# First chunk of a local-and-strided attention with a two-matrix MLP: local exponentials kept in PSUM, copies on another engine, a new order of the opening steps

## The chip, the core and the metric

The kernel runs on one core of a Trainium2 chip. The metric is the device time of one execution in microseconds (us). Three executions of the kernel before took 881.85, 885.22 and 885.75 us; their median is 885.22 us.

## What is computed

```python
scores = q @ k.T / sqrt(64)                       # 8 batches, 8 heads, 576 positions
mask   = local (0 <= i-j < 32) for heads 0..3, strided (i-j >= 0, i%32 == j%32) for heads 4..7
attn   = exp(scores - max); attn = attn / (sum(attn) + 1e-9)
x      = (attn @ v)                               # 4608 tokens x 512
h      = maximum(x @ w_in, 0)                     # 512 x 2048
out    = (h * h) @ w_out                          # 2048 x 512
```

All of it is float32. Products of the MLP are made from split operands: each number is a high part in a rounded format plus the remainder, and a product is three matmuls (high·high, high·low, low·high).

## The kernel before

The 4608 tokens go in twelve chunks of 384. A chunk's MLP has sixteen steps: `up(c, j)` makes 128 rows of h with twelve matmuls of 384 columns (L462), and `down(c, j)` adds them into three PSUM banks with nine matmuls of 512 columns (L489). While TensorE works on chunk c, the other engines prepare the attention of chunk c+1. Between `up` and `down` stand: a relu (L470 in the first chunk), the square (L471, VectorE), the high part `gh` (L475, ScalarE) and the low part `gl` (L476, VectorE).

Nothing can run beside the attention of the first chunk, so it is written apart. Its eight heads are four pairs, each a generator `pe_pair`: `first[0]` and `first[1]` are the local pairs, `late[0]` and `late[1]` the strided ones. A step of a pair runs up to the next `yield`:

1. loads of q and k, then of v (SP's queue);
2. scores by TensorE (L319) and, per window of 96 queries, the negated masked maximum by VectorE (L324, here called a minimum; it also writes the masked scores to SBUF, tile `e`);
3. exponentials and sums. A local pair is `single`: eight ScalarE instructions with an accumulated sum each (L345). A strided pair has its maximum subtracted by GpSimd (L347), two exponentials (L348) and a reduction by VectorE (L349). Then a reduction (L350), a reciprocal (L351) and the division, a multiplication by GpSimd (L353);
4. transposes by TensorE (L359) into the PSUM banks that held the scores, copied to SBUF by ScalarE (L360);
5. the product with v (L367, L378) and the split of the result into x's high part (L382, ScalarE) and low part (L383, VectorE).

The weights arrive as raw pairs of words, 1 MB a tile. `fetch` loads a tile, `convert` turns it into high and low parts in halves of 512 columns: `scale` (L154, ScalarE, 1024 columns), then per half z (L166, ScalarE), a merge (L169, VectorE), the high part (L172, ScalarE) and the low part (L173, GpSimd). L172 and L173 of a half are issued only in the next half's step (`split`).

The order of the opening steps is written by hand (L588 to L628), and a scheduler places instructions of the steps among each other within it, by its own estimate; each engine then runs its own list in order. `issue_after` and `behind` keep what follows behind an instruction. `zeros(bank, n)` issues n matmuls on a tile of zeros into a bank that nobody reads.

Access to a PSUM tile is guarded by the whole bank: a write to one window of it waits for reads of the others.

Of the kernel before, what the change touches and what calls it, by code (L numbers as in the profile page):

```python
# [22 lines left out]
P = 128  # L23
# [63 lines left out]
def attn_moe(ctx: ExitStack, tc, qk_l, v_l, qk_d, v_d, qk_p, v_p, f_s, q_s, k_s, v_s, w_in, w_out, masks, eye, out):  # L87
# [59 lines left out]
    def convert():  # L147
# [9 lines left out]
        for k in range(NFT):  # L157
# [4 lines left out]
            for raw, at in cuts:  # L162
# [8 lines left out]
                def split(w=w, hi=hi, lo=lo, at=at, k=k):  # L171
                    last["a"] = nc.scalar.copy(hi, f32(w))  # L172
                    last["g"] = nc.gpsimd.tensor_sub(lo, f32(w), f32(hi))  # L173
                    if at and 4 <= k < 12:
                        fetch(k + 4)

                if not at and k + 1 < NFT and k + 1 in raws:
                    with tc.issue_after(first_step.ins):
                        scale(k + 1)
# [112 lines left out]
    def pe_pair(c, pr, local, qk, vr, es, pt, banks, sm, single):  # L292
# [22 lines left out]
        s_ps = [banks() for _ in range(2)] if c == 0 else None  # L315
        e4 = [e[:QC, : NW * kw].rearrange("p (w k) -> p w k", k=kw) for e in es]
        def scores(h, w, s):
# [10 lines left out]

        if s_ps:
            for w in range(NW):  # L330
                for h in range(2):
                    scores(h, w, s_ps[h])
# [9 lines left out]
        for h in range(2):  # L342
            if single:
                for w in range(NW):
                    last["a"] = nc.scalar.activation(e4[h][:, w], e4[h][:, w], AF.Exp, bias=nm[:QC, h, w : w + 1], scale=-1.0, accum_out=ss[:QC, NW * h + w, :1])  # L345
            else:
# [5 lines left out]
        for h in range(2):  # L352
            last["g"] = nc.gpsimd.tensor_mul(e4[h], e4[h], rs[:QC, h].unsqueeze(2).broadcast_to([QC, NW, kw]))  # L353
        yield
        p4 = pt.rearrange("p (h w q) -> p h w q", h=2, w=NW)
        for h in range(2):
            t = s_ps[h] if s_ps else banks()
            for w in range(NW):
                nc.tensor.transpose(t[:kw, w * QC : (w + 1) * QC], e4[h][:, w], ident[:QC, :QC])  # L359
            last["a"] = nc.scalar.copy(pt[:kw, h * TC : (h + 1) * TC], t[:kw, :TC])  # L360
        yield
# [241 lines left out]
    with tc.issue_after(last["p"].ins):  # L603
        zeros(0, NWARM // 2)
        for k in range(NEARLY, 8):
            fetch(k)
    next(late[0])
    with tc.issue_after(last["p"].ins):
        zeros(1, NWARM // 2)
    next(first[0])  # L610
    next(first[1])
    weights = behind({"a": last["a"]}, ungated)
    next(late[1])
    for i in range(2):
        next(first[0])
        next(first[1])
        next(late[0])
        next(late[1])
        if i:
            weights = behind({"a": last["a"]}, ungated)  # L620
        for _ in range(2):
            next(weights)
    next(late[0])
    next(late[1])
    for _ in range(2 * NEARLY - 4):
        next(weights)
# [131 lines left out]
```

## Time and profile before

| | |
|---|---|
| median of three executions | 885.22 us |
| the profiled execution: time | 883.18 us |
| the profiled execution: span from first to last instruction | 881.4 us |
| mean granted TensorE clock, share of full | 0.997 |
| TensorE matmuls, share of the span | 99% |
| VectorE | 72% |
| ScalarE | 65% |
| GpSimd | 77% |

The profiled execution lies between the three timed ones, 2.0 us under their median. Busy shares are means over the whole run; the opening, the first chunk and the eleven others have different limits, so the rows that count are those of the first 50 us. Times in rows are us from the start of the span. TensorE's busy share counts pipelined matmuls from issue to end.

### The profile page before, as it was taken

The numbers are of one execution on the slowest core, as the hardware profiler recorded it, in microseconds if no ns is written. First come the engines' busy times: TensorE is split into PE (matmuls) and PEld (weight loads), VectorE is DVE, ScalarE is ACT, GpSimd is POOL, SyncE is SP. The second block draws the span as 40 slices with busy tenths as digits, with TensorE's granted clock in tenths as the row PEclk, the third lists the DMA queues.
The fourth block names the chain that finished last, engine by engine and source line by source line (L and its number), as shares of the span: only waits on it lengthen the run. The fifth ranks groups of instructions, "written<-read, shape, count | busy, mean of one in ns | idle before, by whom it ended". The sixth has DMA issues, their size and how long they took to land.

```text
span 881.4 us, 14862 instructions
## 1 busy us (share of the span) xinstructions
PE 868.5 (99%) x4744; PEld 789.6 (90%) x4744; DVE 635.5 (72%) x1892; ACT 572.6 (65%) x1510; POOL 676.8 (77%) x722
## 2 busy tenths in 40 slices
PE   8899999999999999999999999999999999999997
PEld 7788899999999999999999999999999989998996
DVE  4578687788777888878778778778787787883111
ACT  6798776676676666757657747657666665664332
POOL 4698878878978989898988978997898899782000
PEclk9999999999999999999999999999999999999999
DMA  9851631323123123104102302312131121000000
GB/s 356 355 195 63 184 121 42 103 84 113 32 66 112 37 89 103 44 30 127 44 13 80 115 14 74 104 31 74 31 102 57 30 71 61 7 1 10 28 1 36
DMA packets 26798, 71.41 MB, mean 81 GB/s; under 512 B 2976, under 2 KB 8736, under 8 KB 25184
## 3 DMA queue, kind: packets, MB, share of 16 engines
q1 hardware_dynamic: 26432, 70.14, 23.9%
q8 instruction: 37, 0.61, 0.3%
q10 hardware_dynamic: 288, 0.33, 0.1%
q14 instruction: 41, 0.34, 0.1%
HBM read 61.01 MB, written 9.44 MB: 80 GB/s over the span
## 4 chain that ended last, share of the span: by engine, by line
PE 95%; ACT 3%; DVE 1%; POOL 0%; issue 0%; DVEq 0%; POOLq 0%; ACTq 0%
PE h L462 44%; PE y L489 44%; PE s L234 2%; PE o L280 2%; ACT e L345 1%; PE w_ps L586 1%; ACT raw L154 1%; PE b L319 1%; DVE sc L419 0%; ACT z L166 0%; ACT w L172 0%; DVE raw L169 0%; ACT pt L360 0%; PE b L359 0%; DVE xsl L383 0%
## 5 line engine op out<-in xcount | busy, mean ns | idle before, releaser
L489 PE MATMUL y<-w,gh 128*128 128x512 f32 x1152 | 357.1, 391 | 0.8 <-ACT gh L475 0.8
L489 PEld LDWEIGHTS y<-w,gh 128*128 128x128 f32 x1152 | 212.5, 188 | 41.5 <-ACT gh L475 1.4
L462 PE MATMUL h<-xlh,w 128*128 128x384 f32 x768 | 229.6, 339 | 2.1 <-DVE xsl L383 1.6
L462 PE MATMUL h<-xsh,w 128*128 128x384 f32 x768 | 226.2, 335 | 0.0
L489 PE MATMUL y<-w,gl 128*128 128x512 f32 x576 | 224.0, 392 | 0.0
L434 POOL TENSOR_TENSOR pp<-vs,sc 128x448 f32<-128x448 f32 (+10 forms) x192 | 189.8, 1014 | 39.8 <-DVE qs L435 18.2
L412 POOL TENSOR_TENSOR pq<-ks,qs 128x512 f32<-128x512 f32 (+2 forms) x192 | 197.8, 1050 | 17.9 <-DVE sc L413 13.8
L476 DVE TENSOR_TENSOR gl<-h,gh 128x384 fp32r<-128x384 f32 x192 | 105.4, 550 | 84.2 <-ACT gh L475 82.9
L475 ACT CAST gh<-h 128x384 fp32r<-128x384 f32 x192 | 91.4, 477 | 103.0 <-PE y L489 100.0
L473 ACT ACTIVATE h<-h 128x384 f32<-128x384 f32 x176 | 83.0, 472 | 107.8 <-PE h L462 106.2
L413 DVE TENSOR_REDUCE sc<-pq 128x8 f32<-128x512 f32 (+4 forms) x228 | 119.6, 534 | 46.2 <-POOL pq L412 43.9
L462 PEld LDWEIGHTS h<-xlh,w 128*128 128x128 f32 x768 | 142.1, 188 | 5.6 <-DVE xsl L383 1.8
L462 PEld LDWEIGHTS h<-xsh,w 128*128 128x128 f32 x768 | 141.7, 188 | 0.3
L462 PE MATMUL h<-xll,w 128*128 128x384 f32 x384 | 129.3, 337 | 0.0
L435 DVE TENSOR_REDUCE qs<-pp 128x64 f32<-128x448 f32 (+11 forms) x192 | 106.7, 563 | 31.0 <-POOL pp L434 29.5
L489 PEld LDWEIGHTS y<-w,gl 128*128 128x128 f32 x576 | 108.1, 188 | 22.9
L462 PE MATMUL h<-xsl,w 128*128 128x384 f32 x384 | 128.5, 335 | 0.0
L474 ACT ACTIVATE h<-h 128x384 f32<-128x384 f32 x176 | 83.2, 473 | 3.6
L259 DVE STREAM_TRANSPOSE p_t<-e 32x128 f32<-32x128 f32 x240 | 72.3, 301 | 10.4 <-ACT e L248 6.0
L462 PEld LDWEIGHTS h<-xll,w 128*128 128x128 f32 x384 | 72.5, 189 | 2.2
L462 PEld LDWEIGHTS h<-xsl,w 128*128 128x128 f32 x384 | 72.2, 188 | 0.0
L243 ACT ACTIVATE e<-e,nm 96x128 f32<-96x128 f32 x160 | 62.5, 392 | 10.5 <-DVE nm L226 8.8
(97 smaller groups left out, 1077.2 us busy)
## 6 DMA issues: line engine op xcount, KB each, us to landing
qk<-qk_l SPq DMA_DIRECT2D x24, 400.0 KB, 3.2
y<-ysb SPq DMA_DIRECT2D x36, 256.0 KB, 3.7
raw<-w_in SPq DMA_DIRECT2D x7, 1024.0 KB, 11.2
qk<-qk_l SPq DMA_DIRECT2D x16, 416.0 KB, 3.3
vs<-v_s SPq DMA_DIRECT2D x10, 576.0 KB, 4.0
raw<-w_out SPq DMA_DIRECT2D x5, 1024.0 KB, 12.9
v<-v_l SPq DMA_DIRECT2D x40, 128.0 KB, 2.0
ks<-k_s SPq DMA_DIRECT2D x8, 576.0 KB, 3.8
```

The lines of the kernel that those rows point to most:

```text
L243: nc.scalar.activation(e[:QC, cut(w)], e[:QC, cut(w)], AF.Exp, bias=nmax[:QC, w : w + 1], scale=-1.0, accum_out=ssum[:QC, w, :1])
L259: nc.vector.transpose(out=pt[STR * k : STR * (k + 1), :, STR * r : STR * (r + 1)], in_=e.rearrange("p (w k) -> p w k", k=KW)[STR * r : STR ...
L412: nc.gpsimd.tensor_mul(pv, kt[:, a : a + m, :], qt[:, i - i0 : i - i0 + 1, :].broadcast_to([P, m, D]))
L413: nc.vector.tensor_reduce(out=sc[:, i - i0, a : a + m], in_=pv, op=ALU.add, axis=AX.X)
L434: nc.gpsimd.tensor_mul(pv, vt[:, a : a + nd, :n], sc[:, il : il + 1, :n].broadcast_to([P, nd, n]))
L435: nc.vector.tensor_reduce(out=ot[:, il, a : a + nd], in_=pv, op=ALU.add, axis=AX.X)
L462: done = nc.tensor.matmul(ph[:, :TC], w[:, wsl], xx, start=n == 0, stop=n == 11)
L473: nc.scalar.activation(g, g, AF.Relu)
L474: nc.scalar.activation(g, g, AF.Square)
L475: last["gh"] = nc.scalar.copy(gh, g)
L476: nc.vector.tensor_sub(gl, g, f32(gh))
L489: done = nc.tensor.matmul(y_ps[c][t], g[:, sl], w[:, wsl], start=j == 0 and k == 0, stop=j == NFT - 1 and k == 2)
```

## The change

Four edits, all of the first chunk:

- The exponentials of the local pairs are written into the PSUM bank of their scores (`r4`) and not back to `e`; the division reads that bank and is done by VectorE, which writes `e`.
- The four copies of transposed probabilities of the strided pairs (`pt`, and `w` for the second pair) are made by VectorE; those of the local pairs stay on ScalarE.
- Both strided pairs' scores are issued directly behind the local ones. The two sets of 30 zero matmuls between them go; 12 zero matmuls into 128 unused columns of the last pair's bank come behind the last scores.
- The two halves of the first weight tile are converted in the opening steps ahead of the strided pairs' products, its second half is split at once, and the number of conversion steps behind the opening changes from 2·3−4 to 2·3−2 with two instead of four before it.

```diff
+                if k == 0 and at:
+                    split()
+                    split = None
...
+        r4 = [blocks(t) for t in s_ps] if single else e4
...
+            last["free"] = s_ps[0][:, TC : TC + P]
...
-                    last["a"] = nc.scalar.activation(e4[h][:, w], e4[h][:, w], AF.Exp, bias=nm[:QC, h, w : w + 1], scale=-1.0, accum_out=ss[:QC, NW * h + w, :1])
+                    last["a"] = nc.scalar.activation(r4[h][:, w], e4[h][:, w], AF.Exp, bias=nm[:QC, h, w : w + 1], scale=-1.0, accum_out=ss[:QC, NW * h + w, :1])
...
-            last["g"] = nc.gpsimd.tensor_mul(e4[h], e4[h], rs[:QC, h].unsqueeze(2).broadcast_to([QC, NW, kw]))
+            eng, key = (nc.vector, "v") if single else (nc.gpsimd, "g")
+            last[key] = eng.tensor_mul(e4[h], r4[h], rs[:QC, h].unsqueeze(2).broadcast_to([QC, NW, kw]))
...
-            last["a"] = nc.scalar.copy(pt[:kw, h * TC : (h + 1) * TC], t[:kw, :TC])
+            (nc.vector.tensor_copy if c == 0 and not local else nc.scalar.copy)(pt[:kw, h * TC : (h + 1) * TC], t[:kw, :TC])
...
     with tc.issue_after(last["p"].ins):
-        zeros(0, NWARM // 2)
         for k in range(NEARLY, 8):
             fetch(k)
     next(late[0])
-    with tc.issue_after(last["p"].ins):
-        zeros(1, NWARM // 2)
+    next(late[1])
+    for _ in range(NWARM // 5):
+        nc.tensor.matmul(last["free"], warm, warm, start=True, stop=True)
+    next(first[0])
+    with tc.issue_after(last["a"].ins):
+        next(first[1])
+    weights = behind({"a": last["a"]}, ungated)
     next(first[0])
     next(first[1])
-    weights = behind({"a": last["a"]}, ungated)
+    next(late[0])
     next(late[1])
-    for i in range(2):
-        next(first[0])
-        next(first[1])
+    for _ in range(2):
+        next(weights)
+    next(first[0])
+    next(first[1])
+    for _ in range(2):
         next(late[0])
         next(late[1])
-        if i:
-            weights = behind({"a": last["a"]}, ungated)
-        for _ in range(2):
-            next(weights)
-    next(late[0])
-    next(late[1])
-    for _ in range(2 * NEARLY - 4):
+    weights = behind({"a": last["a"]}, ungated)
+    for _ in range(2 * NEARLY - 2):
         next(weights)
```

ScalarE's list before, from the first exponential on (`e_0_1` is local pair 0, `e_1_1` local pair 1, `e_0_0` and `w_1_0` the strided pairs; a last number tells the two heads apart; in brackets the engine or queue that is waited for):

```order
L345 ACTIVATE e_0_1_109,sums_94<-e_0_1_109,nm_0_1_196 96x128 [waits DVE_49,Pool_49]
L345 ACTIVATE e_0_1_109,sums_94<-e_0_1_109,nm_0_1_196 96x128 [waits DVE_49] x3
L345 ACTIVATE e_0_1_110,sums_94<-e_0_1_110,nm_0_1_196 96x128 [waits DVE_49] x4
L345 ACTIVATE e_1_1_114,sums_95<-e_1_1_114,nm_1_1_216 96x128 [waits DVE_49] x4
L345 ACTIVATE e_1_1_115,sums_95<-e_1_1_115,nm_1_1_216 96x128 [waits DVE_49] x4
L154 ACTIVATE raw_190<-raw_190 128x1024 [waits DMAHW2_49]
L348 ACTIVATE e_0_0_100<-e_0_0_100 96x384 [waits Pool_49]
```

The same place in the changed kernel (its line 352 is line 345 before, 355 is 348; `b_0_1` and `b_1_1` are the PSUM banks):

```order
L352 ACTIVATE b_0_1_198,sums_94<-e_0_1_109,nm_0_1_196 96x128 [waits DVE_49,Pool_49]
L352 ACTIVATE b_0_1_198,sums_94<-e_0_1_109,nm_0_1_196 96x128 [waits Activation_49]
L352 ACTIVATE b_0_1_199,sums_94<-e_0_1_110,nm_0_1_196 96x128 [waits DVE_49]
...
L352 ACTIVATE b_1_1_219,sums_95<-e_1_1_115,nm_1_1_216 96x128 [waits Activation_49]
L355 ACTIVATE e_0_0_100<-e_0_0_100 96x384 [waits Pool_49]
L352 ACTIVATE b_1_1_218,sums_95<-e_1_1_114,nm_1_1_216 96x128 [waits Activation_49]
...
L355 ACTIVATE w_1_0_104<-w_1_0_104 96x384 [waits Pool_49]
...
L154 ACTIVATE raw_190<-raw_190 128x1024 [waits DMAHW2_49]
L355 ACTIVATE w_1_0_104<-w_1_0_104 96x384 [waits Pool_49]
```

The exponentials now wait for ScalarE's own earlier write to the same bank and mostly alternate between two banks; the strided exponentials have moved ahead among and directly behind the local ones (three before the first `scale`, one behind it).

VectorE's list before, between the last minima and the low parts of x (`xll`, `xsl`):

```order
L349 TENSOR_REDUCE sums_94<-w_1_0_104 96x4
L349 TENSOR_REDUCE sums_96<-e_0_0_100 96x4
L169 SCALAR_TENSOR_TENSOR raw_190<-raw_190,z_0_414 128x512
L350 TENSOR_REDUCE rs_0_0_278<-sums_96 96x8
L351 RECIPROCAL rs_0_0_278<-rs_0_0_278 96x8
L383 TENSOR_TENSOR xll_424<-b_0_1_198,xlh_423 128x384
L169 SCALAR_TENSOR_TENSOR raw_190<-raw_190,z_512_418 128x512
```

And in the changed kernel, of the same stretch the part from the second local pair's division on (361 is the division, 368 the copy, 391 is 383 before):

```order
L361 TENSOR_TENSOR e_1_1_114<-b_1_1_218,rs_1_1_217 96x512
L361 TENSOR_TENSOR e_1_1_115<-b_1_1_219,rs_1_1_217 96x512
L356 TENSOR_REDUCE sums_94<-w_1_0_104 96x4
L357 TENSOR_REDUCE rs_1_0_267<-sums_94 96x8
L169 SCALAR_TENSOR_TENSOR raw_190<-raw_190,z_0_364 128x512
L358 RECIPROCAL rs_1_0_267<-rs_1_0_267 96x8
L368 COPY pt_0_0_103<-b_0_0_248 96x384
L169 SCALAR_TENSOR_TENSOR raw_190<-raw_190,z_512_368 128x512
L368 COPY pt_0_0_103<-b_0_0_249 96x384
L391 TENSOR_TENSOR xll_376<-b_0_1_198,xlh_375 128x384
L368 COPY w_1_0_104<-b_1_0_268 96x384
L368 COPY w_1_0_104<-b_1_0_269 96x384
```

Four divisions and four copies have come into VectorE's list ahead of the four `xsl` that the first `up` reads.

VectorE's list at the start of the MLP, before (`sc` and `pq` belong to the next chunk's strided attention, `h` to the first two `up`):

```order
L169 SCALAR_TENSOR_TENSOR raw_194<-raw_194,z_512_526 128x512
L413 TENSOR_REDUCE sc_2_694<-pq_2_0_0_696 128x1
L413 TENSOR_REDUCE sc_2_694<-pq_2_1_0_699 128x2
L471 SCALAR_TENSOR_TENSOR h_0_531<-h_0_531,p_t_90 128x384
L413 TENSOR_REDUCE sc_2_694<-pq_2_2_0_702 128x3
```

And changed:

```order
L169 SCALAR_TENSOR_TENSOR raw_194<-raw_194,z_0_470 128x512
L479 SCALAR_TENSOR_TENSOR h_0_481<-h_0_481,p_t_90 128x384
L479 SCALAR_TENSOR_TENSOR h_1_512<-h_1_512,p_t_91 128x384
L169 SCALAR_TENSOR_TENSOR raw_194<-raw_194,z_512_476 128x512
L484 TENSOR_TENSOR gl_0_495<-h_0_481,gh_0_494 128x384
```

The squares of the first two `up` no longer stand behind reductions of the next chunk.

## Rows read from the trace of the kernel before

**Rows 1.** TensorE's waits, whole run: us in total, times, longest
```profile
PE h L462 <- DVE xsl L383: 1.6, 1, 1.6
PE y L489 <- ACT gh L475: 0.8, 1, 0.8
```
**Rows 2.** Busy us by engine in stretches, granted clock, DMA
```profile
10.00:15.00 5.00, 5.00 (x78) 4.80 (x76) 4.27 (x44) 5.00 (x28) 2.40 (x3) 1.00 1.01 390
...
30.00:35.00 5.00, 4.56 (x18) 4.56 (x19) 2.80 (x5) 4.69 (x9) 2.64 (x2) 0.66 1.01 405
35.00:40.00 5.00, 4.21 (x24) 3.76 (x23) 3.07 (x8) 2.83 (x7) 4.33 (x8) 1.00 1.04 393
40.00:50.00 10.00, 10.00 (x54) 9.31 (x53) 7.48 (x21) 10.00 (x19) 7.24 (x8) 1.00 0.13 50
```
**Rows 3.** Chain that ended last, first 40 us: start, us, what
```profile
21.95 0.43 ACT w L348
...
23.26 0.21 DVE rs L351
...
39.17 2.34 PE y L489 x9
```
**Rows 4.** Timeline, VectorE and ScalarE, the first minima and exponentials: start, us
```profile
8.36 0.29 DVE L324 CUSTOM_DVE_ANT_0 e<-b,mask_sb 96x128 f32<-96x128 f32 x1 [8.36 <-PE b L319]
...
8.58 0.28 DVE L324 CUSTOM_DVE_ANT_0 e<-b,mask_sb 96x128 f32<-96x128 f32 x1
...
8.76 0.40 ACT L345 ACTIVATE e<-e,nm 96x128 f32<-96x128 f32 x1 [6.07 <-DVE nm L324]
...
9.06 0.19 ACT L345 ACTIVATION_READ_ACCUMULATOR e<-e,nm 96x1 f32 x1
...
9.16 0.39 ACT L345 ACTIVATE e<-e,nm 96x128 f32<-96x128 f32 x1
```
**Rows 5.** Timeline, VectorE, minima of the last scores
```profile
17.02 0.24 DVE L324 CUSTOM_DVE_ANT_0 w<-b,mask_sb 96x96 f32<-96x96 f32 x1
...
17.19 0.25 DVE L324 CUSTOM_DVE_ANT_0 w<-b,mask_sb 96x96 f32<-96x96 f32 x1
```
**Rows 6.** Costliest forms, whole run: count, busy us, mean ns, idle before
```profile
L413 DVE TENSOR_REDUCE sc<-pq 128x8 f32<-128x512 f32 x112 | 76.2, 680 | 27.9 <-POOL pq L412 27.0
...
L493 DVE COPY ysb<-y 128x512 f32<-128x512 f32 x24 | 16.4, 685 | 5.2 <-PE y L489 4.5
...
L383 DVE TENSOR_TENSOR xll<-b,xlh 128x384 fp32r<-128x384 f32 x4 | 2.1, 532 | 1.3 <-ACT xlh L382 1.3
```
**Rows 7.** The same, GpSimd, first 40 us
```profile
L353 POOL TENSOR_TENSOR e<-e,rs 96x512 f32<-96x512 f32 x4 | 4.1, 1035 | 9.7 <-DVE rs L351 9.7
```
**Rows 8.** Timeline, all engines, the first steps of the MLP
```profile
30.44 0.69 PE L462 MATMUL h<-xlh,w 128*128 128x384 f32 x1 [1.61 <-DVE xsl L383]
...
37.84 0.29 DVE L413 TENSOR_REDUCE sc<-pq 128x2 f32<-128x128 f32 x1 [0.20 <-POOL pq L412]
...
38.04 0.56 DVE L471 SCALAR_TENSOR_TENSOR h<-h,p_t 128x384 f32<-128x384 f32 x1
...
45.53 0.33 PE L462 MATMUL h<-xlh,w 128*128 128x384 f32 x1
```
**Rows 9.** Timeline, ScalarE, third and fourth step of the MLP
```profile
45.88 0.47 ACT L475 CAST gh<-h 128x384 fp32r<-128x384 f32 x1
46.24 0.50 ACT L470 ACTIVATE p_t<-h 128x384 f32<-128x384 f32 x1
46.62 0.66 ACT L172 CAST w<-raw 128x512 fp32r<-128x512 f32 x1
47.17 0.66 ACT L166 ACTIVATE z<-raw 128x512 uint32<-128x512 uint32 x1
47.73 1.16 ACT L154 ACTIVATE raw<-raw 128x1024 f32<-128x1024 f32 x1
48.77 0.65 ACT L172 CAST w<-raw 128x512 fp32r<-128x512 f32 x1
```

More of the change, by code (lines that the diff above doesn't have):

```diff
@@ L315, in pe_pair @@
         s_ps = [banks() for _ in range(2)] if c == 0 else None
-        e4 = [e[:QC, : NW * kw].rearrange("p (w k) -> p w k", k=kw) for e in es]
+        blocks = lambda t: t[:QC, : NW * kw].rearrange("p (w k) -> p w k", k=kw)
+        e4 = [blocks(e) for e in es]
+        r4 = [blocks(t) for t in s_ps] if single else e4
         def scores(h, w, s):
```

## The prediction

> **What bounds the kernel now.** I read TensorE's waits first. In the whole run it waits for another engine only a few times, and the one large wait ends at the low part of x, ahead of the first `up` [rows 1]; that `up` starts at 30.44 us [rows 8]. Behind it one wait for `gh` is left, which ends at 39.17 us [rows 1, 3]; from there TensorE goes without a pause (10.00 of 10 us busy from 40 to 50 us [rows 2]). So the change can be worth only what it brings forward: the first `up`, then the first `down`, and then whatever of that lead the first chunk doesn't take back. ScalarE, which makes the weights, is full as well from 40 to 50 us [rows 2]; so a lead of TensorE that ScalarE doesn't share is lost.
>
> In the opening the last strided exponential runs only at 21.95 us [rows 3], since its scores' minima start at 17.02 us [rows 5], behind two sets of zero matmuls and behind work on the local pairs.
>
> **The change part by part.** All starts at the first minimum, 8.36 us [rows 4], which nothing in the change moves.
>
> *Exponentials in PSUM.* The first one now waits for four minima instead of one, as the bank is guarded as a whole: minima follow each other by 0.21–0.22 us (8.36, 8.58 [rows 4]), so it starts 0.63 us later, at 9.39 us. Exponentials follow by 0.39–0.40 us (8.76, 9.16 [rows 4]). Where two of one bank stand next to each other (two places, by the lists), the second waits for the end of the first: its accumulator is read 0.30 us after its start and takes 0.19 us [rows 4], so 0.49 us and some 0.05 us for the signal, 0.15 us more than the spacing. Two places cost 0.3 us; the bounds are zero, if the wait is already served, and 16 × 0.15 = 2.4 us, if alternating banks don't hide it. I take 0.3, since an exponential two places back has ended long before. Sixteen exponentials and the three strided ones among them (0.43 us each [rows 3]) end at 9.39 + 16 × 0.39 + 0.3 + 3 × 0.43 = 17.2 us; the first `scale` (1.04 us, the step from 47.73 to 48.77 [rows 9]) and the last strided one follow, to 18.6 us. Before, that one ended at 22.4 us.
>
> *Divisions on VectorE.* They take four times 1.035 us off GpSimd [rows 7] and put four operations of 512 columns on VectorE. The trace has no division from PSUM. The nearest rows are a 512-column copy out of PSUM, 0.685 us, and from below a 384-column subtraction out of PSUM, 0.532 us [rows 6]; from above GpSimd's own 1.035 us. I take 0.685: 2.74 us.
>
> [...]
>
> *Last scores sooner.* The strided minima (0.18 us each: 17.02, 17.19 [rows 5]) come directly behind the local ones: 8.36 + 16 × 0.21 + 16 × 0.18 = 14.6 us instead of 17.9. The 60 zero matmuls that go, and the 12 that come, stand on no chain by themselves; TensorE was full with them from 10 to 15 us [rows 2], and what they covered is a rival below.
>
> *Copies on VectorE and weights ahead.* ScalarE loses four copies, VectorE gains four of 384 columns (0.53 us by the nearest row [rows 6]; between 0.5 and 0.685). The loads of the weights keep their place on SP; the loads of the next chunk's v now stand behind a division and are wanted some 40 us later, so they cost nothing. GpSimd has room: it waited 9.7 us for the first division [rows 7].
>
> *The sum.* VectorE is now the engine with the longest list, so I add it: minima to 14.6; one reduction (0.2 us, as the reciprocal [rows 3]), 14.8; then, to the first weight merge, four divisions 2.74, four sums 2.1 and six small ones 1.2: 20.9; two merges of 512 columns, two copies and a reciprocal, 2.6: 23.5 us. Next it takes the first x, which ScalarE must have rounded: ScalarE goes from 18.6 through four copies (0.38 us each, as the relu from 46.24 to 46.62), two z and two casts (0.55, as from 46.62 to 47.17) and one `scale` [rows 9], 4.8 us, with 0.4 for waits 5.2, and the cast of x itself, 0.48 [rows 9], to 24.3. So VectorE waits 0.8 us here, then has two low parts and two copies (2.1), and two `xsl` (1.1): the first `up` at 27.5–27.6 us, where TensorE waits for the second `xsl`. That is **2.8 us sooner** than 30.44.
>
> Now the first `down`. ScalarE follows with two more `xsl` to wait for and then, each behind its merge, three z and three casts, one `scale` and two relus at the same prices: `gh` of step 0 starts at 34.9 us. The square ahead of it stood at 38.04 us behind a reduction of the next chunk that waited for GpSimd [rows 8]; it no longer does. First `down` at 35.4 us, 3.8 sooner than 39.17. That lead isn't kept: the scheduler put the sixth `up` where it needs the low part of the third, and ScalarE has to do four z, three casts, two `scale`, two relus and one `gh` before that `gh`: 7.4 us by [rows 9], so it starts at 42.35, its low part ends at 43.3. TensorE then stands where it stood at 45.53 + 0.35 = 45.88 us before (two matmuls into the fifth `up`) [rows 8]. **The lead left is 2.5 us.** From here the lists of both kernels carry the same work, and I let 2.5 us stand.
>
> The profiled execution took 883.18 us: 880.7. It lies 2.0 us under the median of the three timed ones, 885.22, from which it is 882.7. I forecast 882.6 us. Within 0.5% (4.4 us) is about what a measurement of this kernel can't tell from no change, so this forecast is "the same".
>
> **Rivals.**
>
> *More is kept (faster).* If ScalarE reaches the third `gh` sooner than I add (a placement cheaper by 0.02 us per exponential, no wait at the sixth `up`), the lead at the first `down`, 3.8 us, stays, and if the 0.5–1 us of small waits in the first chunk go too it is 4.5 us: 880.7 from the median. For it speaks that every engine starts its list earlier; against it that ScalarE was full from 40 to 50 us [rows 2].
>
> *VectorE becomes the bound.* A division at GpSimd's 1.035 us and a copy at 0.685 add 4 × 0.35 + 4 × 0.15 = 2.0 us to a list that has only 0.8 us of waits in it: first `up` at 28.8, and the same delay at `gh`; or ScalarE's load in the first chunk takes the lead back, down to some 1 us. Time 884.4. For it: VectorE's list has nearly no gap from 8.4 to 23.5.
>
> *TensorE's clock (slower).* [...] Without the zero matmuls TensorE has nothing to do from the last scores to the 12 new ones, which wait for minima near 14 us, and then small pieces. If its clock falls there, its short steps on the chain double, for which I allow 1 us, and the first `up`s run at half speed: each 3.4 us at that level costs 1.7 us. One such stretch is in the time before already. It decides once the stretch lasts over 5 us longer than before: with 1 us in the opening and 2 × 1.7 = 3.4 us more in the first three `up`s, less 2.5, it ends 1.9 us slower: 887.1.
>
> [...]
>
> *It doesn't do what it says.* If the exponentials are served one after the other (2.4 us above), the strided ones slip with them and the first `up` comes at 29.5: 884.6, in with the second rival.
>
> **How the numbers follow.** Forecast (gain 1 to 3.5 us) 0.40; more is kept 0.26; VectorE or ScalarE takes most of it, or the waits do, 0.23; clock 0.11. Likeliest 882.6. The three runs before spread over 3.9 us, and the range takes that in on both sides: 879.0 to 887.0, from the first rival less 1.7 to the clock's 887.1; the forecast's own range is 881 to 884.5. Faster than 880.8: two thirds of the first rival and a quarter of the forecast, 0.28. Slower than 889.6: half of the clock's case, where it lasts longer still, 0.06. The same: 0.66.
>
> **What would show it.** First `up` near 27.6 us, waiting for `xsl`; divisions near 0.69 us on VectorE; exponentials 0.39 us apart but for two; `gh` of step 0 near 34.9 and a wait of TensorE ahead of the sixth `up` near 41.5–43.4. Wrong, if the first `up` is later than 29 us, if TensorE shows several waits in the first chunk, or if the granted clock is at the lower level before the first `up` and long after it.

## The result, and the profile after: 2.5 us slower

| | before | changed |
|---|---|---|
| median | 884.47 us (20 executions) | 886.97 us (20 executions) |
| lowest to highest | 881.85 to 886.27 us | 884.89 to 889.3 us |
| profiled execution: time, span | 883.18, 881.4 us | 887.1, 885.3 us |

The ratio is 1.0028, 95% interval 1.0021 to 1.0035. The forecast was 882.6 us.

The first view is TensorE's waits in the changed kernel, to be set against [rows 1] (waited for, us in total, times, longest):

```profile
PE b L618 <- DVE nm L330: 3.5, 1, 3.5
PE h L470 <- POOL xsl L454: 1.6, 1, 1.6
...
PE h L470 <- DVE gl L484: 1.3, 1, 1.3
PE b L367 <- ACT w L355: 1.1, 1, 1.1
PE y L497 <- ACT gh L483: 1.0, 1, 1.0
```

The wait for `xsl` ahead of the first `up` is gone. In its place stand one for minima early on (by the 12 zero matmuls), one for a `gl`, and one for another `xsl`, that of line 454, which belongs to the second chunk.

Next, stretches of the opening (us, then busy time of TensorE and its weight loads, VectorE, ScalarE, GpSimd, and the granted clock behind them), to be set against [rows 2]:

```profile
10.00:14.00 4.00, 1.11 (x27) 1.04 (x25) 4.00 (x44) 3.94 (x20) 0.83 (x2) 1.00 1.00 387
14.00:15.00 1.00, 0.36 (x4) 0.36 (x4) 1.00 (x13) 1.00 (x7) 1.00 (x2) 0.60 1.00 418
15.00:20.00 5.00, 3.35 (x23) 2.63 (x20) 5.00 (x17) 4.97 (x16) 2.75 (x4) 0.50 1.01 416
20.00:25.00 5.00, 5.00 (x31) 3.52 (x30) 2.57 (x7) 4.53 (x8) 3.54 (x5) 0.50 1.01 419
25.00:30.00 5.00, 5.00 (x44) 4.07 (x44) 2.46 (x5) 0.48 (x1) 0.86 (x1) 0.50 1.02 424
30.00:31.50 1.50, 1.50 (x32) 1.50 (x30) 0.55 (x1) 0.61 (x2) 0.00 (x0) 0.58 0.99 398
31.50:35.00 3.50, 3.38 (x36) 3.16 (x31) 2.27 (x4) 3.39 (x6) 0.00 (x0) 1.00 1.02 405
```

The granted clock falls from 1.00 to 0.50 at 14.2 us, inside the wait of 3.5 us, and comes back to 1.00 at 31.3 us. From 20 to 30 us TensorE is full, and from 25 to 30 us ScalarE (0.48 of 5 us) and GpSimd (0.86) are nearly idle: before, TensorE waited for the others in this stretch (6.61 of 10 us busy); now the others wait for it.

TensorE's timeline at the places that the prediction spoke of (start, us, what, and in brackets the idle time before):

```profile
14.63 1.44 PE L618 MATMUL b<-p_t 128*128 128x128 bf16 x12 [3.52 <-DVE nm L330]
...
32.48 0.45 PE L470 MATMUL h<-xlh,w 128*128 128x384 f32 x1
...
40.53 0.97 PE L497 MATMUL y<-w,gh 128*128 128x512 f32 x3 [1.02 <-ACT gh L483]
...
48.73 0.45 PE L470 MATMUL h<-xlh,w 128*128 128x384 f32 x1 [1.34 <-DVE gl L484]
```

The first `up` starts at 32.48 us, 2.0 later than before [rows 8], the first `down` 1.4 later [rows 3]: the first `up`s, which before ran partly at the low clock (0.50 up to 33.5 us), now run at full clock (1.00 from 31.5 to 35 us). Of both, 0.55 us are a later start of the opening, told below. Then the wait of 1.34 us for a `gl` comes on top, and near 110 us the one for `xsl`.

The engines that the prediction reckoned with did nearly what it said. ScalarE's first exponentials and its last strided one:

```profile
9.94 0.37 ACT L352 ACTIVATE b<-e,nm 96x128 f32<-96x128 f32 x1 [7.26 <-DVE nm L330]
...
10.47 0.37 ACT L352 ACTIVATE b<-e,nm 96x128 f32<-96x128 f32 x1
...
10.87 0.35 ACT L352 ACTIVATE b<-e,nm 96x128 f32<-96x128 f32 x1
...
18.63 0.52 ACT L355 ACTIVATE w<-w 96x384 f32<-96x384 f32 x1
```

All of it lies 0.55 us later than forecast, since the first minimum does (8.91 us, against [rows 4]). That isn't the change: the first scores stand in TensorE's list behind the 60 zero matmuls at the start, which took 6.27 us here, 5.72 in the profiled execution before and 5.10 in another execution of the changed kernel (a_again, first minimum at 7.74). The first pair of exponentials, in one bank, is 0.53 apart, the next two 0.40. The last strided one starts at 18.63 us; before, at 21.95 [rows 3]. VectorE's new operations (count, busy us, mean ns, to be set against [rows 6, 7]):

```profile
L361 DVE TENSOR_TENSOR e<-b,rs 96x512 f32<-96x512 f32 x4 | 2.6, 679 | 0.0
...
L368 DVE COPY pt<-b 96x384 f32<-96x384 f32 x2 | 1.1, 554 | 1.6 <-PE b L367 1.5
```

679 ns is the price that was taken (685). The division is by that no dearer out of PSUM than the 680 ns of 512 columns out of SBUF [rows 6], though the two rows are different operations.

What was reckoned too low is the price of TensorE's small pieces at the lower clock (0.50). Two batches of products with v and one of transposes, first 32 us, in the changed kernel:

```profile
L375 PE MATMUL b<-pt,v 128*64 128x96 f32 x32 | 4.5, 378 | 0.0
L386 PE MATMUL b<-pt,v 96*32 96x96 f32 x32 | 3.3, 368 | 0.0
L367 PE MATMUL b<-ident,e 96*128 96x96 f32 x16 | 3.3, 374 | 1.6 <-ACT w L355 1.1 <-ACT e L355 0.6
```

and in a kernel of the experiments whose code differs in zero matmuls alone and which keeps its clock there (1.00, a_zeros_30_30):

```profile
L375 PE MATMUL b<-pt,v 128*64 128x96 f32 x32 | 2.1, 254 | 1.1 <-ACT pt L368 1.1
L386 PE MATMUL b<-pt,v 96*32 96x96 f32 x32 | 2.1, 250 | 0.2
...
L367 PE MATMUL b<-ident,e 96*128 96x96 f32 x16 | 1.9, 253 | 0.7 <-ACT b L352 0.6
```

Each of these batches takes 1.2 to 2.4 us longer.

Last, GpSimd's list around the second chunk's last `xsl`, in the changed kernel:

```profile
103.01 1.15 POOL L221 TENSOR_TENSOR kx<-qk,kx 128x448 fp32r<-128x448 f32 x1
104.13 1.79 POOL L442 TENSOR_TENSOR pp<-qkvs,sc 128x320 f32<-128x320 f32 x2
106.00 1.01 POOL L223 TENSOR_TENSOR qx<-qk,qx 64x384 fp32r<-64x384 f32 x1
107.09 0.73 POOL L258 TENSOR_TENSOR vx<-v,vx 128x256 fp32r<-128x256 f32 x1
...
109.90 0.73 POOL L420 TENSOR_TENSOR pq<-qkvs 128x64 f32<-128x64 f32 x2
110.59 1.00 POOL L454 TENSOR_TENSOR xsl<-qkvs,xsh 128x384 fp32r<-128x384 f32 x1
```

and in the kernel before:

```profile
102.86 1.02 POOL L446 TENSOR_TENSOR xsl<-qkvs,xsh 128x384 fp32r<-128x384 f32 x1
...
106.07 1.16 POOL L218 TENSOR_TENSOR kx<-qk,kx 128x448 fp32r<-128x448 f32 x1
107.31 1.01 POOL L220 TENSOR_TENSOR qx<-qk,qx 64x384 fp32r<-64x384 f32 x1
```

`kx`, `qx`, `vx` and `pq` there belong to the third chunk. The changed kernel has all four ahead of `xsl`, the kernel before none.

The theory: two losses, the low clock from 14 to 31 us, and the new place of that `xsl`. The rival: only one of them costs, the other goes along with it.

### The profile page after: what moved, and what is told of

Same layout as the page of the kernel before. It is cut to its first block, busy times and chain, and to the rows that moved or that the text cites. A ratio compares the mean times of both kernels' runs of the same rounds, so it can differ in the third digit from the quotient of the medians.

```text
span 885.3 us, 14775 instructions
## 1 busy us (share of the span) xinstructions
PE 869.7 (98%) x4696; PEld 789.6 (89%) x4696; DVE 638.0 (72%) x1900; ACT 571.1 (65%) x1506; POOL 673.1 (76%) x718
## 4 chain that ended last, share of the span: by engine, by line
PE 95%; POOL 2%; ACT 1%; DVE 1%; issue 1%; DVEq 0%; POOLq 0%
PE h L470 44%; PE y L497 44%; PE s L237 2%; PE o L283 2%; PE w_ps L594 1%; PE b L367 1%; PE b L325 1%; PE b L375 1%; DVE e L330 0%; PE b L386 0%; POOL w L173 0%; ACT raw L154 0%; ACT z L166 0%; POOL pq L420 0%; POOL pp L442 0%
## 5 line engine op out<-in xcount | busy, mean ns | idle before, releaser
L442 POOL TENSOR_TENSOR pp<-vs,sc 128x448 f32<-128x448 f32 (+10 forms) x192 | 189.8, 1014 | 38.9 <-DVE qs L443 18.6
```

The source lines that it names most:

```text
L442: nc.gpsimd.tensor_mul(pv, vt[:, a : a + nd, :n], sc[:, il : il + 1, :n].broadcast_to([P, nd, n]))
```

## The experiments

"Before" beside each is the kernel before, run on the same chip. Every execution also has its mean granted clock over the span; where executions of one kernel part by it, that is told. Where a time is given at which the clock falls or comes back, it is worked out from the means of the stretches, with 0.50 for the low and 1.00 for the full clock, and is good to some 0.1 us.

**Zero matmuls out of the kernel before (b_no_zeros).**

```diff
-        zeros(0, NWARM // 2)
...
-        zeros(1, NWARM // 2)
```

> The kernel before without the two sets of 30 zero matmuls ahead of the strided scores; all other code is as before (the lists of the engines shift a little with it: the strided minima come sooner). Clock theory (the zero matmuls held TensorE's clock): the granted clock falls to 0.5 between 12 and 17 us and stays there up to 28 us or longer, the first up starts at 31.5 us or later, and the time is 1 to 4 us above the kernel before. Rival (the changed kernel lost by the new order of its lists, the clock is a side effect): the first up starts at 30.4 us or sooner, as the strided scores come sooner, and the time is within 1 us of before or below it.

885.78 against 884.07 us, ratio 1.0018 (1.0007 to 1.0029). TensorE's two largest waits in its trace:

```profile
PE b L359 <- POOL e L353: 6.3, 1, 6.3
PE y L489 <- ACT gh L475: 2.4, 1, 2.4
```

Without the zero matmuls the wait of 6.3 us is bare. Two stretches behind it:

```profile
15.00:20.00 5.00, 3.19 (x16) 2.23 (x18) 2.93 (x11) 4.35 (x9) 5.00 (x6) 0.50 1.01 418
20.00:25.00 5.00, 5.00 (x35) 4.30 (x36) 1.77 (x3) 4.06 (x9) 4.04 (x5) 0.50 1.02 423
```

The clock falls as the theory has it and the loss is of the size it gave; but the first `up` starts at 30.13 us, not behind 31.5; that sooner scores paid for part is likely and not shown. The loss shows at the first `down` (39.62 us, 0.45 later than before), ahead of which TensorE waits the 2.4 us for `gh`, and behind it: the clock falls once more and is at 0.50 from 40.1 to 43.5 us.

**Zero matmuls back into the changed kernel (a_zeros_30_30, a_zeros_8_24).**

```diff
     with tc.issue_after(last["p"].ins):
+        zeros(0, 30)     # 8 in a_zeros_8_24
         for k in range(NEARLY, 8):
             fetch(k)
     next(late[0])
+    with tc.issue_after(last["p"].ins):
+        zeros(1, 30)     # 24 in a_zeros_8_24
     next(late[1])
```

> The changed kernel with the two sets of 30 zero matmuls back at the places where the kernel before has them. Clock theory: granted clock 1.00 from 10 to 27 us, transposes and small products at the old durations (4 transposes 0.54 us, not 0.87), first up at 27.5 to 29.0 us, time 1 to 3.5 us below before, so 881 to 883.5 where before is 884.5. Rival (order of the lists, waits behind 40 us): the first up comes sooner than 32.5 but the waits for gl near 48 us (1.3) and for xsl near 110 us (1.6) are there still, and the time is 884 to 887.

> The changed kernel with 8 zero matmuls ahead of the first strided pair's scores and 24 ahead of the second's, besides the 12 it has; here ScalarE's and GpSimd's lists of the opening stay nearly as in the changed kernel (one strided exponential moves by five places). Clock theory: granted clock 1.00 to some 25 us, first up at 27.5 to 29.5 us, time 881 to 884 where before is 884.5. Rival (order of the lists): first up sooner, but TensorE waits behind 40 us as in the changed kernel, and 884 to 887.

885.66 and 885.85 against 884.07 us, ratios 1.0027 (1.0014 to 1.0039) and 1.0026 (1.0012 to 1.0041). In both the clock theory alone fails on the time. In the profiled execution the 30 and 30 hold the clock at 1.00 from 10 to 100 us and bring the first `up` to 29.19 and the first `down` to 37.79 us, 1.3 and 1.4 sooner than before; all of that and more is lost near 107 us, at a wait that has grown. In a_zeros_30_30's list of waits:

```profile
PE h L470 <- POOL xsl L454: 2.5, 1, 2.5
```

It was 1.6. The stretches around it show a second fall of the clock:

```profile
106.00:108.00 2.00, 0.00 (x0) 0.00 (x0) 0.00 (x0) 0.00 (x0) 2.00 (x2) 1.00 0.86 264
108.00:110.00 2.00, 1.82 (x8) 1.82 (x9) 0.77 (x2) 0.54 (x2) 2.00 (x4) 0.78 0.82 210
110.00:112.00 2.00, 2.00 (x9) 1.93 (x8) 1.30 (x4) 0.96 (x3) 1.16 (x2) 0.50 0.94 378
```

From 106 to 108 us every engine but GpSimd is idle. With 8 and 24 the clock still fell, for some 6.8 us between 15 and 25 us (0.68 and 0.64 in its two stretches), and the waits for `gl` (1.3) and `xsl` (1.5) are those of the changed kernel.

**The place of `xsl` (a_zeros_gate, a_zeros_xsl_dve, a_gate).** In the first and the third the third chunk's preparations wait for it; in the second VectorE makes it. The first two have the 30 and 30 zero matmuls, the third has not.

```diff
-            nc.gpsimd.tensor_sub(x["s", "l"][:, :, cols], ...)
+            last["xs"] = nc.gpsimd.tensor_sub(x["s", "l"][:, :, cols], ...)
...
-    for i in (last["pe"], *(weights_end.values() if c == NPLAIN else ())):
+    for i in (last["pe"], *([*weights_end.values(), last["xs"]] if c == NPLAIN else ())):
```
```diff
-            nc.gpsimd.tensor_sub(x["s", "l"][:, :, cols], ...)
+            (nc.vector if c == 1 else nc.gpsimd).tensor_sub(x["s", "l"][:, :, cols], ...)
```

> The changed kernel with 30 and 30 zero matmuls back, and with the two preparations of the third chunk's heads (kx, qx, vx on GpSimd) kept behind the low part xsl of the second chunk's last strided piece. Theory (the rest of the loss is xsl standing in GpSimd's list behind the third chunk's work): xsl at 103 to 105 us instead of 107.1, TensorE waits for it less than 0.7 us instead of 2.5, granted clock 1.00 from 100 to 120 us, time 2.5 to 4 us below a_zeros_30_30 and so 881.7 to 883.2 where before is 884.1. Rival (GpSimd as a whole is the bound, the order in its list only moves the wait): a wait of the same length stands later, at the third chunk's heads, and the time is 884.5 to 886.

> The changed kernel with 30 and 30 zero matmuls back, and with the low part xsl of the second chunk's strided pieces made by VectorE, not GpSimd. Theory: xsl follows its transposes on VectorE, near 101 to 104 us, no wait of TensorE for it over 0.5 us, granted clock 1.00 from 100 to 120 us, time 881.7 to 883.2 where before is 884.1. Rival (GpSimd as a whole is the bound): 884.5 to 886 with a new wait behind 104 us.

> The changed kernel, without more zero matmuls, and with only the third chunk's kx, qx and vx kept behind that xsl. Both theories are taken apart here: the low clock of the opening stays (first up near 32.5 us), the wait for xsl near 110 us goes for the most part. If the two losses simply add, the time is 1 to 2 us below the changed kernel: 885 to 886 where before is 884.1. If the clock alone explains the loss, it is unchanged: 886.5 to 887.5.

881.47, 881.25 and 883.72 against 884.0 us; ratios 0.9972 (0.9961 to 0.9983), 0.9967 (0.9957 to 0.9977) and 0.9999 (0.999 to 1.0008). With the clock held, the place alone is worth 4.2 us: the wait of 2.5 and the low clock behind it. GpSimd's timeline in a_zeros_gate:

```profile
104.48 1.01 POOL L454 TENSOR_TENSOR xsl<-qkvs,xsh 128x384 fp32r<-128x384 f32 x1
105.45 1.15 POOL L221 TENSOR_TENSOR kx<-qk,kx 128x448 fp32r<-128x448 f32 x1
```

`kx` now follows `xsl`. What TensorE still waits for it:

```profile
PE h L470 <- POOL xsl L454: 0.2, 1, 0.2
```

And the stretch as a whole, where the clock was 0.91 in a_zeros_30_30:

```profile
100.00:120.00 20.00, 19.63 (x100) 17.23 (x99) 13.64 (x54) 14.84 (x44) 14.17 (x20) 1.00 0.60 187
```

So `xsl` comes 2.7 us sooner (104.48 against 107.14), the wait is 0.2, the clock stays, and no new wait of such a length stands behind it. GpSimd as a whole is not the bound. In a_gate the clock is low in the opening, as in the changed kernel, and it gains all the same, more than its expectation had (883.72, expected 885 to 886).

Two of these are better than both kernels: a_zeros_xsl_dve and a_zeros_gate, 0.33% and 0.28% faster than the kernel before. They are called the mended kernels below.

**The engines' edits alone (b_engines).** The kernel before with `r4`, VectorE's divisions and VectorE's copies, in the old order of steps.

> The kernel before with the exponentials in PSUM, VectorE's divisions and VectorE's copies alone; the order of the opening steps, the zero matmuls and the conversions are those of before. Its GpSimd list has xsl of the second chunk behind kx, qx and vx of the third, as in the changed kernel, though the clock is held by the zero matmuls. Theory (xsl's place costs by itself): granted clock 1.00 to 28 us, first up 29 to 30.5, a wait for xsl of 1 to 2.5 us near 110 us, time 884.5 to 886.5. Rival (only the low clock costs): no loss, 882 to 884.

884.88 against 884.0 us, ratio 1.001 (1.0001 to 1.0018). The time falls into the theory's range, for another reason. There is no wait for `xsl` among TensorE's, though it starts at 108.01 us, since TensorE gets to it only at 109.07. The clock, expected at 1.00 to 28 us, fell at 24.4 (0.94 on average from 20 to 25 us), behind waits of 0.83 and 0.25 us at 22 to 23.5 us, and the first `up` starts at 31.82. The two stretches from there:

```profile
25.00:30.00 5.00, 5.00 (x53) 3.95 (x54) 3.32 (x6) 4.69 (x8) 3.63 (x3) 0.50 0.99 409
30.00:35.00 5.00, 5.00 (x35) 4.72 (x32) 2.97 (x5) 4.14 (x8) 2.25 (x3) 0.53 1.01 407
```

So here the same zero matmuls didn't keep it; the fall came behind the waits that follow them.

**The changed kernel once more (a_again).**

> The changed kernel once more, unchanged, beside the others on one chip, to see how far its opening and its two late waits repeat. Theory: clock 0.5 from 14 to 26 us or longer in this profile too, first up between 30.5 and 33 us (its place depends on when the clock comes back), the wait for xsl of 1.4 to 1.8 us near 110 us again, time 886 to 887.5. Rival (the profiled execution was an outlier): first up before 30.4 or no wait for xsl, time 884 to 885.5.

885.66 against 884.17 us, ratio 1.0019 (1.001 to 1.0029). The clock is low again (0.52, 0.50 and 0.62 in the three stretches from 15 to 30 us), the waits for `gl` and `xsl` are there again (1.4, 1.5); the first `up` starts at 30.71 us, 1.8 sooner than in the other profiled execution, and the time of the profiled execution is 1.8 us shorter (885.3 against 887.1). Of that, 1.2 us are the sooner start of the opening (first minimum at 7.74 against 8.91 us), so the shorter stretch at the low clock (13.7 us, 15.2 to 28.9, against 17.1) is left with some 0.6.

**`xsl` late in the kernel before (b_late_xsl).** Its last part is issued at the end of the first chunk and kept behind the third chunk's first `kx` and `qx`.

```diff
+        last["qx"] = nc.gpsimd.tensor_sub(qx[D:], qr[D:], f32(qx[D:]))
...
+            late_x = c == 1 and b == ranges(1)[-1][0]
+            if late_x:
+                yield 1000
+            with ExitStack() as st:
+                if late_x:
+                    st.enter_context(tc.issue_after(last["qx"].ins))
-            nc.gpsimd.tensor_sub(x["s", "l"][:, :, cols], ...)
+                nc.gpsimd.tensor_sub(x["s", "l"][:, :, cols], ...)
```

> The kernel before, with one thing added: the low part xsl of the second chunk's last strided piece is kept behind kx and qx of the third chunk's first head in GpSimd's list (a place like that in the changed kernel). Theory: xsl starts near 107 to 109 us instead of 102.86; TensorE reads it 1.2 us into the second chunk, near 106.4, so it waits 1.5 to 3.5 us there; the time is 1.5 to 4 us above before, 885.5 to 888. Rival (the place of xsl in the list is harmless, what costs is GpSimd's load): a wait under 0.5 us and a time within 0.7 us of before.

886.31 against 884.17 us, ratio 1.0018 (1.0006 to 1.0031). It doesn't decide: `xsl` started at 106.61 us, and the wait was only 0.5 us; the time is in the theory's range, but seven of its eleven executions had a mean clock of 0.990 or less, against some third of the kernel before's, and a wait of 0.5 us doesn't explain that.

**The new order without the engines' edits (a_order_gate).** a_zeros_gate with exponentials back in SBUF, GpSimd's divisions and ScalarE's copies.

> The mended changed kernel (30 and 30 zero matmuls back, the third chunk's kx, qx and vx behind xsl), but with the local exponentials written to SBUF, GpSimd's divisions and ScalarE's copies, as before: of the change only the order of the steps and the weights ahead are left. Theory (the lead comes from the engines' edits, which take 4.1 us off GpSimd's part of the chain): first up 0.8 to 2.5 us later than the 28.9 of the mended kernel, time 882.3 to 884.3. Rival (the new order alone brings it): first up 28 to 29.5 us, time 881 to 882.

882.24 against 884.17 us, ratio 0.9978 (0.9969 to 0.9988). That lies between what the two sides expected. By the ratios the edits on the engines are worth 0.5 us, by the medians 0.8. The first `up` starts at 27.28 us, sooner than with them, but the first `down` only at 38.23 (37.47 with them), so it isn't through the first `up` that they pay.

**More zero matmuls behind the last scores (a_free_30 and a_free_30b, a_free_60; a_free_30_gate, a_free_60_gate).** This is the cleanest test, since the other engines' lists stay nearly those of the changed kernel. The last two have the gate on `kx`, `qx`, `vx` as well.

```diff
-    for _ in range(NWARM // 5):
+    for _ in range(30):     # or 60
         nc.tensor.matmul(last["free"], warm, warm, start=True, stop=True)
```

> The changed kernel with 30 instead of 12 zero matmuls behind the last scores; the lists of the other engines are the same but for two neighbours each. They still wait for the last minima, so TensorE is idle from 11.1 to 14.6 us as in the changed kernel, and the clock is low when they start. Clock theory: they run at half speed to 18 us; if their activity lifts the clock again the first up comes at 28.5 to 31 us and the time is 883 to 886.5; if not, the first up comes at 32.5 to 34 and the time is 886.5 to 888.5. Rival (TensorE's own list of the opening is too long, whatever the clock): later by the 2 us that 18 more of them take, 888 to 889.

> The same kernel as a_free_30 (30 zero matmuls behind the last scores; the other engines' lists are those of the changed kernel but for a few neighbours). Its ten executions before fell into two groups: five with a mean granted clock of 0.985 to 0.992 took 886.6 to 887.9 us, five with 0.996 to 0.998 took 881.7 to 882.2. Theory (the low clock of the opening is the whole loss against the forecast): the two groups come again, and the group at 0.996 or more takes 881.5 to 883, the forecast's 882.6; should the profiled execution be of that group, its first up starts at 27.5 to 29 us. Rival (the place of xsl costs in either state): the good group takes 884 us or more.

> The changed kernel with 60 instead of 12 zero matmuls behind the last scores; lists of the other engines as in the changed kernel but for a few neighbours. They take 3.7 us at full clock, so the first pair's transposes, due near 16 us, wait 1.5 to 2.5 us for them. Theory (clock): more executions hold the clock than with 30; those at 0.996 or more have the first up at 28 to 30.5 us and take 882 to 884; the median is below before's 884.1. Rival (the zero matmuls stand in the way more than the clock gives): median 884.5 to 887.

> a_free_30 with the third chunk's kx, qx and vx kept behind xsl. What is open is whether xsl's place costs anything with the changed kernel's own lists once the clock is held. If it does (theory of two causes): executions at 0.996 or more take 880 to 881.3, about 1.5 us less than a_free_30's 882. If the clock is all: 881.7 to 882.5, as a_free_30. Executions at the low clock: 883 to 885.3, as a_gate.

> a_free_60 with the third chunk's kx, qx and vx kept behind xsl: the version that could hold the clock in most executions and loses nothing at xsl. Two causes: executions at 0.996 or more take 880.5 to 882.5, the median is below 883. Clock alone: as a_free_60, 882 to 884. It beats a_zeros_gate (881.5) only if the transposes lose less than 1 us behind the 60 zero matmuls.

Medians 884.42 and 884.55, 883.55, 885.45 and 882.0 us; only the last is apart from before (0.9969, 0.9957 to 0.9981). With 30 the executions fall into two groups, and the medians say only how many fell into which; so here the groups are shown (median, lowest to highest in us, count):

| lists | mean clock 0.996 or more | mean clock 0.992 or less |
|---|---|---|
| changed kernel (with a_again) | none | 886.7 (884.9 to 889.3), 32 |
| a_free_30 and a_free_30b | 882.1 (881.7 to 882.4), 11 | 887.7 (886.6 to 888.1), 11 |
| a_gate | none | 883.7 (883.0 to 885.3), 12 |
| a_free_30_gate | 880.4 (880.2 to 880.5), 3 | 886.0 (884.8 to 886.1), 9 |

With 30, down a column the gate is worth 1.7 us in either group (882.1 to 880.4, 887.7 to 886.0); along a row the clock is worth 5.6 us. There the two causes stand apart and add. With the changed kernel's 12 the table has 3.0 us for the gate (886.7 to 883.7), but the opening varies: against a_again, on the same chip, it is 1.9 (885.66 to 883.72), and the two profiled executions, whose clock is low over nearly the same stretch (15.2 to 28.9 and 15.4 to 29.1 us), are 1.7 apart (885.3 and 883.64). Against the changed kernel itself (886.7) the faster group of a_free_30 is ahead by 4.6 us, not 5.6; the slower group is 1.0 us behind the changed kernel.

No execution of a faster group with 30 was profiled, so how the clock goes in one isn't shown. Two of the slower group were profiled with a_free_30's lists. One has the fall at 13.5 us, inside the wait of 3.52 us for the minima, and the return at 37.4. In the other the 30 run at full clock behind the same wait, and the fall comes at 18.1, behind a further wait of 1.43 us. The slower group of a_free_30_gate lies above the range expected (883 to 885.3). With 60, no execution of 21 was under 0.995; their times (882.1 to 885.0, with the gate 880.1 to 883.3) are near the ranges expected. The profile of a_free_60 shows the clock low from 12.4 us and back at 19.2, and its first `up` starts at 29.49:

```profile
15.00:20.00 5.00, 5.00 (x54) 5.00 (x53) 4.27 (x12) 3.28 (x10) 2.08 (x3) 0.58 1.01 416
20.00:25.00 5.00, 5.00 (x61) 3.78 (x60) 2.79 (x7) 4.78 (x10) 1.61 (x2) 1.00 1.02 423
```

With 12 in that place it stayed low to 31 us, in a_again to 29.

**The kernel before with its clock held (b_hold).** 24 zero matmuls into a free bank ahead of the conversions behind the opening.

```diff
+    zeros(2, 24)
     for _ in range(2 * NEARLY - 4):
         next(weights)
```

> The kernel before with 24 zero matmuls more, into a bank that is free between the last products of the opening and the second up; lists behind them shift by some places. In the kernel before TensorE waits 1.6 us ahead of the first up and the clock falls at 30 us. If the mended kernel (881.5) owes its gain to the clock alone, this one, with a mean granted clock of 0.999 or 1.0, takes 880.5 to 882. If the new order and the engines' edits are worth 1.5 us or more at equal clock, it takes 883 or more at that clock. If the clock still falls (mean under 0.996), it stays at 883.5 to 886 and tells nothing of that.

882.65 against 884.79 us, ratio 0.9982 (0.9973 to 0.9991): 1.6 us, somewhat over half of what the mended kernels gain. None of its eleven executions had a mean clock under 0.994, of the fifteen of the kernel before beside it eight were at 0.991 or less; that speaks for the clock. But only one had 1.0, as the expectation asked; it took 881.91 us. The profiled one (0.998) still has 0.66 from 30 to 35 us, as the kernel before, and yet its first `down` comes 1.0 us sooner (38.17 us), so the lists have changed with it; and it has a new wait of 1.3 us for the second chunk's `xsl`. How much of the gain of the mended kernels is the clock, and what the new lists add at equal clock (0.4 us by that one execution, about 1 by these ratios), is not settled.

## Why the prediction was wrong

*The step that failed* is the one on the zero matmuls: "The 60 zero matmuls that go, and the 12 that come, stand on no chain by themselves". They were costed at nothing, and their cover was left to a rival. What they covered is TensorE's clock. Without them TensorE waits 3.52 us from 11.1 us on, the clock falls, and it stays at 0.50 for some 17 us (14.2 to 31.3), though TensorE is full from 20 to 30. That the clock is what costs is shown with nearly the same lists and 30 zero matmuls: 5.6 us between the two groups (887.7 and 882.1), 4.6 against the changed kernel itself. That 882.1 is near the forecast's 882.6 is luck: those executions still have the late `xsl`, and without it they took 880.4, under the forecast's own range.

The rival on the clock gave 887.1 and measured is 886.97, but its working was off as well: it put 1 us into the opening and 3.4 into the first `up`s, and had nothing for the second chunk's `xsl`; that its number fits is luck too. In the trace the first `up`s run at full clock, and the loss lies in transposes and products ahead of them (the three batches shown 2.4, 1.2 and 1.4 us). The stretch of 3.4 us that it reckoned with is in the trace of before (below), and the price of 1.7 us for it comes to 1.6, an estimate from the same trace: matmuls of 384 columns follow each other by 0.32 us from 30.93 to 33.17 us, at 0.50, and by 0.17 from 33.87 to 36.30 us, at 1.00. That short steps double is not shown: the three batches took 2.1, 1.6 and 1.7 times as long. That the clock falls without the zero matmuls was right, and its chance, 0.11, far too small: all 32 executions of the changed kernel had a mean clock of 0.992 or less. The sign was in [rows 2]: a low clock behind a wait of 1.6 us. In finer stretches of the same trace:

```profile
29.75:30.00 0.25, 0.00 (x0) 0.00 (x0) 0.16 (x1) 0.23 (x2) 0.04 (x1) 1.00 0.92 379
30.00:30.25 0.25, 0.00 (x0) 0.00 (x0) 0.25 (x1) 0.25 (x2) 0.00 (x0) 0.72 0.83 340
30.25:30.50 0.25, 0.06 (x1) 0.06 (x1) 0.22 (x2) 0.25 (x2) 0.00 (x0) 0.50 0.87 356
...
33.25:33.50 0.25, 0.25 (x3) 0.25 (x2) 0.25 (x1) 0.25 (x2) 0.06 (x1) 0.50 1.06 418
33.50:33.75 0.25, 0.25 (x3) 0.25 (x3) 0.08 (x1) 0.25 (x1) 0.22 (x1) 0.96 1.01 398
```

That is 0.50 from 30.1 to 33.5 us. The change made a wait of 3.5.

More zero matmuls were followed by a higher clock: in a_free_60 and a_free_60_gate it comes back from 0.50 to 1.00 while the 60 run, at 19.2 and 17.4 us; and with 30 instead of 12 of them 14 executions of 34 had a mean clock of 0.996 or more, with 60 all 21 had 0.995 or more.

*The second step that failed* is "From here the lists of both kernels carry the same work, and I let 2.5 us stand". The same work, but not in the same order: the scheduler put `xsl` behind the third chunk's preparations, 70 us behind the part that was read closely. That costs 1.7 to 1.9 us with the changed kernel's lists and 4.2 with those of a_zeros_30_30, where TensorE comes sooner and waits longer: a lead that arrives at a late buffer is given back there.

*Point by point.* Exponentials: their spacing (0.40 and 0.53), the last strided one (it starts at 18.63 us, forecast 18.2, its end at 18.6 less 0.43; the difference is the later start of the opening), the divisions' price, the first weight merge (20.59, forecast 20.9) were right. First `up` 27.6: 32.48; with the clock held or soon back 28.5 to 29.5. First `down` 35.4: 40.53; with the clock held or soon back 37.1 to 37.8. So the sum was short too, in the profiled a_zeros_gate by 1.4 us up to the first `up` and 2.2 up to the first `down`, both counted from the first minimum. It put the last `xsl` straight behind VectorE's last copies; in a_zeros_gate TensorE first makes 30 products from them, from 27.41 us on, and goes into the first `up` at 28.85 without a wait for `xsl`. Where the other 0.8 us lie is open. A wait ahead of the sixth `up`: right in kind and size (1.34), at 48.7 instead of 43. That VectorE would be the longest list: it was not; from 20 to 30 us TensorE was. The new self-waits cost what was said: the accumulator's read ends at 10.44 us and the next exponential in that bank starts at 10.47, 0.03 us behind it, for which the prediction's 0.05 was its author's estimate. Besides the wait for `gh`, the kernel before has one more behind the first `up`, of 0.5 us for a `gl` at 89.6 us, which the prediction passes over. First `up` behind 29 us and a low clock before it were named as what would show the forecast wrong, and did.

The base was uncertain as well. The kernel before has the same illness in part: of 139 executions of it beside the experiments, 51 had a mean clock of 0.991 or less (median 885.3 us), 65 had 0.996 or more (883.6). The profiled one had 0.997.

## What to carry to other kernels

Matmuls that compute nothing may be what holds TensorE's clock (here 1.00 from 10 to 100 us in a_zeros_30_30, 0.50 from 14.2 to 31.3 us in the changed kernel): before they are taken out, look at how long TensorE then waits and what it does next, and price the matmuls that follow at the lower clock (here 17 us, in which three batches took 1.6 to 2.1 times as long). Where a scheduler places instructions, a lead is kept only if the next few things that TensorE reads come sooner as well, so follow each engine's list to the first use of the next chunk, not only to the end of the edit. And where times of one kernel scatter by some 4 us, sort the executions by granted clock before their medians are compared.

## What was not expected of the hardware

- The clock fell late in a run as well, behind a single wait: in a_zeros_30_30 TensorE is without a matmul for 2.5 us up to 108.2 us, the clock falls 1.0 us later and stays at 0.50 for 3.4 us, though TensorE had been full from 50 to 100 us.
- The same lists go one way or the other: of 22 executions of a_free_30 and a_free_30b 11 had a mean clock of 0.996 or more and 11 of 0.992 or less, 5.6 us apart, with nothing between 882.4 and 886.6 us.
- ScalarE's exponential of 128 columns took 354 ns on average into PSUM (390 to 400 into SBUF [rows 4]), so writing it there cost that engine nothing here but where two in a row wrote the same bank (0.53 instead of 0.40 us apart).
